# Four adjacent PSUM banks as one tile for a Strassen-type kernel's products, and sums of seven blocks handled as wide operations

## The chip, the cores and the metric

The kernel runs on one core of one Trainium2 chip. The metric is the device time of one execution in microseconds. Three runs of the kernel before took 747.97, 747.55 and 747.0 us, so the median is 747.55 us. The engines are named as the profile names them: PE multiplies (PEld loads its weights), DVE does elementwise vector work, ACT copies and applies functions, POOL does a little housekeeping, SP issues transfers. Products land in PSUM, which has eight banks of 512 fp32 columns in each of 128 partitions.

## What is computed

The reference, cut to what matters, with 8 batches, 8 heads, 576 tokens, head size 64, a model width of 512 and a hidden width of 1024, all in fp32:

```
kv  = einsum('bhsd,bhse->bhde', k, v)
out = einsum('bhsd,bhde->bhse', q, kv)
x   = out / sqrt(mean(out*out, -1) + 1e-6) * g_norm      # then heads side by side: 4608 x 512
a, b = x @ w1, x @ w2
return ((a * b) @ w3) @ w_out
```

## The kernel before

The kernel first multiplies w3 by w_out once (`fold_chunk`, L682: w3o, 1024 x 512, eight sums in two halves of four PSUM banks), because the two last products have nothing between them. Then it goes through nine groups T of 512 tokens: the first 512 of each of the batches 0 to 7, and group 8, which collects the 64 left-over tokens of each batch. The order is 0 to 6, 8, 7. Each group has two stages: the gates, `a * b` for 1024 hidden columns in four parts p0 to p3, and the projection by w3o. Attention for the next batch (k times v, L335; q times kv, L413; left-over tokens, L432) is done in between, in pieces that a list in `steps` places.

Matrix products are not done plainly but with Winograd's form of Strassen's scheme: seven products of quarter blocks and a chain of sums and differences. `winograd` (L705 for its matmuls) runs one level of it. Its seven products are accumulated in three PSUM banks r1, r2, r3, since several of the sums can be made by letting PE add onto what a bank holds: after product 1, ACT copies r1 to SBUF (`keep`, L719, name p1); product 3 is added onto r1 and is copied again (u2); product 5 is added onto r1 and, in most parts, copied (u3); product 7 is added too. Products 2 and 4 share r2, and product 6 has r3. Each result c12, c22, c11, c21 is then a sum of a bank and an SBUF copy, made by DVE (L848) and followed by the multiplication a*b (L849); for c21 ACT copies one half of r1 (L843) and DVE multiplies it with the other half (L845).

From group 1 on the projection (`project_twice`, L1175), and from group 2 on half of the gates (`gates_of_two`, L964, for the parts p0 and p1 together), use two levels: each of the seven products is itself seven small products of 128 x 128, which land as seven blocks in two PSUM banks, four in the first and three in the second. ACT copies them in two instructions (L984 and L985, L1186 and L1187), or DVE adds them onto an SBUF copy in two (L989 and L990, L1214 and L1215), and `finish` turns a sum of seven blocks into a quarter result with four DVE operations (L1001 to L1004, L1196 to L1199), and for the second factor of the gates multiplies (L1006). The inner sums of the left operand are made by DVE in `sum_inner` (L1133 to L1137), four operations for each of the seven products.

The order on PE, POOL and SP is that of the source (`manual_schedule`); in the last part of the gates and the projection that holds for DVE too. Elsewhere a scheduler orders DVE and ACT. Semaphore waits between engines are put in by the framework, which follows who writes and reads which tile. `between` pieces put attention work behind the third and sixth product of a level; `run_slot` puts ACT's half of the transposes behind a certain copy.

PSUM is shared by two pools: `ps_mm` has five tiles of one bank for products, `ps_at` three for attention. Each `bank(ps_mm, "mm")` is a tile of its own and takes over the bank of an older tile once that has been read:

```
    ps_mm = ctx.enter_context(tc.tile_pool(name="ps_mm", bufs=5, space=PSUM))
    ps_at = ctx.enter_context(tc.tile_pool(name="ps_at", bufs=3, space=PSUM))
    def bank(pool, tag):
        return pool.tile([P, 512], FP32, name=tag, tag=tag)
```

## Time and profile before

| what | value |
|---|---|
| median of three runs | 747.55 us |
| span of the profiled execution | 744.3 us |
| what the median has beyond that span | 3.25 us |
| PE busy | 736.6 us, 99% |
| DVE busy | 648.0 us, 87%, 1377 instructions |
| ACT busy | 379.3 us, 51%, 652 instructions |
| mean granted TensorE clock | 1.000 |
| DMA moved | 169.67 MB, mean 228 GB/s |

The profiled execution's own span is 744.3 us from the first to the last instruction; the time of a run has some 3 us of start and end around it. The stages lie as follows in the span: the fold of w3 and w_out to 82.7 us, group 0 to 149, group 1 to 238, groups 2 to 6 about 73 us each to 604.6, groups 8 and 7 about 68 us each, without attention. PE's matmuls count as busy from issue to their modelled end, so that neighbours overlap by some 0.16 us; an fp32 matmul of 128 x 128 starts every 0.223 us and one of 128 x 256 every 0.432 us when nothing holds them (98 of the former in 21.89 us, 24 of the latter in 10.36 us).

### The profile page before, as it was taken

The page shows a single profiled execution, that of the slowest core. Times are in us where ns is not written, and L with a number is a line of the kernel's source. Part 1 is how long each engine was busy: PE and PEld are TensorE (multiplying, and loading weights), DVE is VectorE, ACT ScalarE, POOL GpSimd, SP SyncE. Part 2 cuts the span into 40 slices and gives each one's busy share as a digit, 9 for nine tenths or more (in the row PEclk, how much of TensorE's full clock was granted, in tenths as well). Part 3 has the DMA queues.
Part 4 walks back from the last instruction along what each step waited for, and adds up shares of the span by engine and source line. Part 5 has one row for each costly group of instructions (what it writes and reads, how often), then busy time and mean ns, then how long its engine had stood idle before and what let it go on. Part 6 is the DMA issues. An engine that isn't in the chain of part 4 may idle for free.

```text
span 744.3 us, 16995 instructions
## 1 busy us (share of the span) xinstructions
PE 736.6 (99%) x6843; PEld 657.9 (88%) x6843; DVE 648.0 (87%) x1377; ACT 379.3 (51%) x652; POOL 22.4 (3%) x29
## 2 busy tenths in 40 slices
PE   8999999999999999999999999999999999999998
PEld 5455788888899999999999999999999999999997
DVE  7987998967869798989898989898989997898897
ACT  6787868415553575356536753575267323222421
POOL 0000000132000000010000000000001000000000
PEclk9999999999999999999999999999999999999999
DMA  9997934499997789678967896679757662465454
GB/s 316 367 304 220 256 103 126 122 337 301 285 294 291 213 221 274 264 200 244 276 237 208 255 291 243 213 240 264 254 141 220 215 217 87 163 227 163 135 198 136
DMA packets 135458, 169.67 MB, mean 228 GB/s; under 512 B 78036, under 2 KB 110804, under 8 KB 135380
## 3 DMA queue, kind: packets, MB, share of 16 engines
q1 hardware_dynamic: 132928, 154.16, 68.0%
q10 hardware_dynamic: 2452, 14.42, 5.6%
q8 instruction: 54, 0.88, 0.5%
q14 instruction: 24, 0.20, 0.1%
HBM read 130.55 MB, written 20.71 MB: 203 GB/s over the span
## 4 chain that ended last, share of the span: by engine, by line
PE 95%; DVE 2%; DMA 2%; ACT 0%; issue 0%; SPq 0%; ACTq 0%; DVEq 0%
PE mm L705 37%; PE mm L1175 23%; PE mm L964 21%; PE mm L682 7%; PE at L335 2%; PE at L413 1%; DMA raw<-in_moe_w_out_dram 1%; PE mm L413 1%; PE at L669 1%; DVE ab L162 1%; DVE w_sb L172 0%; PE at L1226 0%; DMA raw<-in_moe_w_dram 0%; DVE c L848 0%; PE at L432 0%
## 5 line engine op out<-in xcount | busy, mean ns | idle before, releaser
L705 PE MATMUL mm<-xT,w_sb 128*128 128x256 f32 x480 | 110.2, 379 | 0.0
L705 PEld LDWEIGHTS mm<-xT,w_sb 128*128 128x128 f32 x480 | 90.3, 190 | 12.2 <-issue 0.5
L705 PE MATMUL mm<-xc,ws 128*128 128x256 f32 x352 | 79.6, 379 | 0.0
L705 PEld LDWEIGHTS mm<-xc,ws 128*128 128x128 f32 x352 | 66.9, 190 | 9.1
L682 PE MATMUL mm<-chunks,ab 128*128 128x512 f32 x128 | 60.7, 605 | 0.7 <-DVE chunks L172 0.7
L964 PE MATMUL mm<-ws,w3o_sb 128*128 128x128 f32 x350 | 53.9, 275 | 0.0
L719 ACT COPY u<-mm 128x512 f32<-128x512 f32 x38 | 22.3, 586 | 58.0 <-PE mm L705 31.0
L1186 ACT COPY u<-mm 128x512 f32<-128x512 f32 x23 | 13.5, 586 | 75.3 <-DVE raw L1199 44.0
L1175 PE MATMUL mm<-w3o_sb,ab 128*128 128x128 f32 x368 | 48.6, 275 | 0.0
L719 ACT COPY p<-mm 128x512 f32<-128x512 f32 x46 | 27.0, 588 | 41.6 <-PE mm L705 26.6
L1175 PE MATMUL mm<-w3o_sb,raw 128*128 128x128 f32 x372 | 48.1, 275 | 0.0
L964 PEld LDWEIGHTS mm<-ws,w3o_sb 128*128 128x128 f32 x350 | 46.4, 192 | 0.0
L1175 PEld LDWEIGHTS mm<-w3o_sb,ab 128*128 128x128 f32 x368 | 45.4, 192 | 0.4
L1175 PEld LDWEIGHTS mm<-w3o_sb,raw 128*128 128x128 f32 x372 | 44.8, 192 | 0.0
L705 PE MATMUL mm<-xc,w_sb 128*128 128x256 f32 x176 | 42.5, 384 | 0.9 <-ACT u L719 0.9
L381 DVE TENSOR_REDUCE inv<-sq 128x8 f32<-128x512 f32 (+1 forms) x40 | 24.6, 629 | 21.1 <-ACT sq L380 21.1
L682 PEld LDWEIGHTS mm<-chunks,ab 128*128 128x128 f32 x128 | 21.6, 190 | 22.4 <-issue 14.4
L705 PE MATMUL mm<-xT,ws 128*128 128x256 f32 x160 | 38.5, 384 | 0.0
L705 PEld LDWEIGHTS mm<-xc,w_sb 128*128 128x128 f32 x176 | 32.7, 190 | 6.2 <-ACT u L719 1.7
L843 ACT COPY c<-mm 128x256 f32<-128x256 f32 x22 | 8.2, 371 | 53.9 <-PE mm L705 53.9
L308 ACT COPY xT<-xn 128x1024 uint16<-128x1024 uint16 x28 | 32.5, 1168 | 2.3 <-DMA xn<-xT 2.3
L705 PEld LDWEIGHTS mm<-xT,ws 128*128 128x128 f32 x160 | 29.8, 190 | 4.2
(250 smaller groups left out, 1745.9 us busy)
## 6 DMA issues: line engine op xcount, KB each, us to landing
w3o_sb<-w_l SPq DMA_DIRECT2D x21, 896.0 KB, 5.4
w3o_sb<-w3o_l SPq DMA_DIRECT2D x18, 896.0 KB, 5.1
raw<-in_moe_w_dram SPq DMA_DIRECT2D x31, 512.0 KB, 7.6
raw<-w3o_l SPq DMA_DIRECT2D x15, 896.0 KB, 4.7
w3o_sb<-w3o_l ACTq DMA_DIRECT2D x14, 896.0 KB, 5.0
k_sb<-in_k_dram SPq DMA_DIRECT2D x16, 576.0 KB, 4.7
v_sb<-in_v_dram SPq DMA_DIRECT2D x16, 576.0 KB, 5.9
q_sb<-in_q_dram SPq DMA_DIRECT2D x32, 256.0 KB, 3.5
```

The source lines that it names most:

```text
L162: nc.vector.scalar_tensor_tensor(out=low_bits, in0=hi, scalar=0x80000000, in1=low_bits, op0=ALU.bitwise_and, op1=ALU.bitwise_or,)
L308: copy(words(dst), src)
L335: nc.tensor.matmul(ps[r * D:(r + 1) * D, :], lhsT=k_sb[rows, r, cols], rhs=v_sb[rows, r, cols], start=(j == 0), stop=(j == JS - 1),)
L381: adds["norm"] = nc.vector.tensor_reduce(out=inv[:, i], in_=sq.rearrange("p (h d) -> p h d", d=D), axis=AX.X, op=ALU.add)
L413: nc.tensor.matmul(o_ps[l][tokens, n * D:(n + 1) * D], lhsT=qT[r][rows, e, i, tokens], rhs=kv_b[rows, m // 2 ^ l, e, h, :], start=True, st ...
L682: nc.tensor.matmul(sums_ps[half][m], lhsT=w3T[half, c][:, m, :], rhs=chunks[:, c, 1, :], start=(c == 0), stop=(c == KF - 1),)
L705: nc.tensor.matmul(ps[:, u, :], lhsT=lhsT(a_name, u, c), rhs=rhs(b_name, c),  start=(u == 0 and c == 0 and to is None), stop=(c == chunks ...
L719: copies.setdefault(name, []).append(nc.scalar.copy(t, ps))
L843: copied = nc.scalar.copy(c, one[:, 0, :])
L964: nc.tensor.matmul(ps[place // 4][:, place % 4, :], lhsT=x, rhs=y, start=new and place // 4 not in seen, stop=True, skip_group_check=True,)
L1175: nc.tensor.matmul(to[:, i, :], lhsT=x[:, c, :], rhs=y[:, c, :], start=new and place // 4 not in seen, stop=(c == 1), skip_group_check=True,)
L1186: nc.scalar.copy(t[:, 0:4], ps[0])
```

## The change

The five product tiles of one bank become one tile `mm` of four adjacent banks, allocated once, and the attention pool gets four banks. A counter (`next_unit`) alternates between the two halves. A `winograd` takes both banks of its half for r1 and r2 and the second bank of the other half for r3; the two-level stages use one half for r1 and the other for r2, so that seven blocks are 896 adjacent columns and are copied or added in one instruction each. The SBUF copies live in three adjacent slots, so that two of them can be finished by one set of wide operations (`finish_two_sums`); `sum_inner` makes the inner sums for two products at a time where their operands are adjacent; `sum_ab_two` covers three parts instead of two. In the gates the second factor's result is made in place in its slot. k times v of the next batch moves from the last part of the gates of groups 2 to 5 to the place of the batch's second attention product. All attention products use the attention pool. The multiplications, their operands and their order on PE are otherwise the same: 3466 matmuls before and after. The diff, cut to its core (the same edits to `keep`, `add` and `finish` are made in `project_twice`):

```diff
-    ps_mm = ctx.enter_context(tc.tile_pool(name="ps_mm", bufs=5, space=PSUM))
-    ps_at = ctx.enter_context(tc.tile_pool(name="ps_at", bufs=3, space=PSUM))
+    ps_mm = ctx.enter_context(tc.tile_pool(name="ps_mm", bufs=1, space=PSUM))
+    ps_at = ctx.enter_context(tc.tile_pool(name="ps_at", bufs=4, space=PSUM))
+    mm = ps_mm.tile([P, 4, 512], FP32, name="mm")
+    def next_unit():
+        units.append(len(units) % 2)
+        return units[-1]
+    def two_banks(k):
+        return mm[:, 2 * k:2 * k + 2, :].rearrange("p b (i n) -> p (b i) n", n=P)
...
-    ab = [const.tile([P, NF, 2, N], FP32, name=f"ab{i}") for i in range(2)]
+    ab_all = const.tile([P, 2, NF, 2, N], FP32, name="ab")
+    ab = [ab_all[:, i] for i in range(2)]
...
-            sums_ps[half] = [bank(ps_mm, "mm") for m in range(NH)]
+            sums_ps[half] = [mm[:, m, :] for m in range(NH)]
...
         if more:
-            fs[6 if in_two else second].append((batch(b + 1).begin_kv, 0))
+            fs[second].append((batch(b + 1).begin_kv, 0))
...
     # winograd
-            ps = to if to is not None else bank(ps_mm, "mm").rearrange("p (u n) -> p u n", u=2)
+        unit = next_unit()
+        r1, r2, r3 = (
+            mm[:, i, :].rearrange("p (u n) -> p u n", u=2)
+            for i in (2 * unit, 2 * unit + 1, 2 * (1 - unit) + 1)
+        )
...
     # gates_of_two
-            nc.scalar.copy(t[:, 0:4], ps[0])
-            run_slot(at, nc.scalar.copy(t[:, 4:7], ps[1][:, 0:3]))
+            run_slot(at, nc.scalar.copy(z, ps[:, 0:7]))
...
-            nc.vector.tensor_add(z[:, 0:4], ps[0], z[:, 0:4])
-            nc.vector.tensor_add(z[:, 4:7], ps[1][:, 0:3], z[:, 4:7])
+            nc.vector.tensor_add(z, ps[:, 0:7], z)
...
-            r1, r3, r2 = ([mm[i] for i in pair] for pair in plan[w])
+            unit = next_unit()
+            r1, r2 = two_banks(unit), two_banks(1 - unit)
...
+    def finish_two_sums(z, dst, multiply=False):
+        def wide(i):
+            return z[:, :, i:i + 1].to_broadcast([P, 2, 2, P])
+        ...
+        nc.vector.tensor_add(z[:, :, 6], z[:, :, 6], z[:, :, 0])
+        nc.vector.tensor_add(z[:, :, 4:6], z[:, :, 4:6], wide(6))
+        nc.vector.tensor_add(to_1, z[:, :, 1:3], wide(4))
+        last = nc.vector.tensor_add(to_0, z[:, :, 3:6:2], z[:, :, 0:3:2])
...
-        c11, c12, c21, c22 = (ab[i][:, 0:2, j, :] for i in range(2) for j in range(2))
-        s1, s2, s4 = (t[:, 0:2] for t in ab_sums)
+        c11, c12, c21, c22 = (ab[i][:, 0:NF - 1, j, :] for i in range(2) for j in range(2))
+        s1, s2, s4 = (t[:, 0:NF - 1] for t in ab_sums)
...
     # the last part of the gates
-                        lambda: sum_inner(0, lambda: all_of(f() for f in (sum_2, sum_3))),
-                        lambda: sum_inner(1),
+                        lambda: sum_inner(0, between=lambda: all_of(f() for f in (sum_2, sum_3))),
+                        lambda: sum_inner(1, 2),
...
                     following["c22"].append(of_two[0])
-                    following["c21"].append(of_two[1])
+                    following["c11"].insert(1, of_two[1])
```

More of the change, by code (lines that the diff above doesn't have):

```diff
@@ L85, in bank @@
         return pool.tile([P, 512], FP32, name=tag, tag=tag)
+    mm = ps_mm.tile([P, 4, 512], FP32, name="mm")
+    units = []
+    def next_unit():
[3 more added lines that the diff above has]
+        return mm[:, 2 * k:2 * k + 2, :].rearrange("p b (i n) -> p (b i) n", n=P)
     loaded, copies, adds = {}, {}, {}
@@ L271, in keep_warm @@
     def keep_warm(n):
-        t = bank(ps_mm, "mm")
+        t = bank(ps_at, "at")
         for _ in range(n):
@@ L399, in product @@
         def product(h):
-            of_mm = b and not (h and b > FIRST_OF_TWO)
-            o_ps = [bank(*((ps_mm, "mm") if of_mm else (ps_at, "at"))), bank(ps_at, "at")]
+            o_ps = [bank(ps_at, "at") for _ in range(2)]
             for m in range(4):
@@ L570, in turns_by_scalar @@
                 at(("p3", "u2"), begin, ("q", b + 1, r), n.q_by_dma, r)
-                at(("proj", ("u2", "u3")[r]), end, ("q", b + 1, r))
+                at(("proj", "u2"), end, ("q", b + 1, r))
     def steps(b):
@@ L691, with late_slots @@
     tick = const.tile([P, 1], FP32, name="tick")
-    def late_tile(name):
-        return late_pool.tile([P, 7, P], FP32, name=name[0] if name[0] == "u" else name)
+    sums_in_slots = []
+    def late_slots(a, n=1):
+        return sums_in_slots[0][:, a] if n == 1 else sums_in_slots[0][:, a:a + n]
     def winograd(
@@ L698, in winograd, with product @@
     ):
-        def product(a_name, b_name, to=None):
-            ps = to if to is not None else bank(ps_mm, "mm").rearrange("p (u n) -> p u n", u=2)
+        unit = next_unit()
[3 more added lines that the diff above has]
+        )
+        def product(a_name, b_name, ps, new=True):
             for u in range(2):
@@ L708, in product @@
                         rhs=rhs(b_name, c),
-                        start=(u == 0 and c == 0 and to is None),
+                        start=(u == 0 and c == 0 and new),
                         stop=(c == chunks - 1),
@@ L714, in product @@
             after()
-            return ps
         def keep(name, ps):
-            t = late_tile(name)[:, 0:4, :].rearrange("p (u a) n -> p u (a n)", u=2)
+            if name == "p1":
+                t = pair_of_sums[:, 0].rearrange("p s c t -> p (s c) t")
+            else:
+                t = late_slots(2 if name == "p5" else 1)
+            t = t[:, 0:4, :].rearrange("p (u a) n -> p u (a n)", u=2)
             copies.setdefault(name, []).append(nc.scalar.copy(t, ps))
@@ L722, in keep @@
             return t
-        r1 = product("a11", "b11")
+        product("a11", "b11", r1)
         p1 = keep("p1", r1)
-        r2 = product("s1", "t1")
+        product("s1", "t1", r2)
         p5 = keep("p5", r2)
-        product("s2", "t2", r1)
+        product("s2", "t2", r1, False)
         u2 = keep("u2", r1)
         between()
-        product("s4", "b22", r2)
+        product("s4", "b22", r2, False)
         done("c12", r2, u2)
-        product("s3", "t3", r1)
+        product("s3", "t3", r1, False)
         done("c22", p5, keep("u3", r1) if keep_u3 else r1)
-        r3 = product("a12", "b21")
+        product("a12", "b21", r3)
         done("c11", r3, p1)
         between()
-        product("a22", "t4", r1)
+        product("a22", "t4", r1, False)
         done("c21", r1, None)
@@ L772 @@
     o_sbs, ab_sums, w3o_sums, streams, inner_sums, in_a_row = [], [], [], [], [], []
+    two_ab_sums, two_o_sbs = [], []
     PART = 7 * 2 * P
@@ L779, in allocate @@
             free["w", p] = late_pool.tile([P, 3, 2, h, P], FP32, name=f"ws{p}")
+        sums_in_slots.append(late_pool.tile([P, 3, 7, P], FP32, name="slots"))
     def allocate_projection():
@@ L788, in allocate_projection @@
         ab_sums.extend(blocks[0:3])
+        two_ab_sums.append(room[0].rearrange("p (s f n) -> p s f n", s=2, n=N))
         w3o_sums.extend(blocks[3:6])
         o_sbs.extend(t.rearrange("p (m j) t -> p m (j t)", m=2) for t in blocks[6:8])
+        two_o_sbs.append(room[3].rearrange("p (h m n) -> p h m n", h=2, m=2))
         for p in range(NF):
@@ L936, in gates_of_two @@
     def gates_of_two(T, between=lambda: None):
-        mm = [bank(ps_mm, "mm").rearrange("p (i n) -> p i n", n=P) for _ in range(5)]
-        plan = [((0, 1), (2, 3), (4, 2)), ((3, 4), (2, 0), (1, 2))]
-        names = [("p1", "p5", "u2", "p1"), ("u2", "p5", "p1", "u2")]
+        places = [(0, 1, 2, 0), (2, 0, 1, 2)]
         def products(n, w, ps, new):
@@ L964, in products @@
                 nc.tensor.matmul(
-                    ps[place // 4][:, place % 4, :], lhsT=x, rhs=y,
+                    ps[:, place, :], lhsT=x, rhs=y,
                     start=new and place // 4 not in seen, stop=True, skip_group_check=True,
@@ L971, in products @@
                 between()
-            return ps
         def load(w, n):
@@ L980, in load, with keep @@
                     load_b()
-        def keep(name, ps, at):
-            t = late_tile(name)
-            nc.scalar.copy(t[:, 0:4], ps[0])
-            run_slot(at, nc.scalar.copy(t[:, 4:7], ps[1][:, 0:3]))
-            return t
+        def keep(slot, ps, at):
+            z = late_slots(slot)
+            run_slot(at, nc.scalar.copy(z, ps[:, 0:7]))
+            return z
         def add(z, ps):
-            nc.vector.tensor_add(z[:, 0:4], ps[0], z[:, 0:4])
-            nc.vector.tensor_add(z[:, 4:7], ps[1][:, 0:3], z[:, 4:7])
+            nc.vector.tensor_add(z, ps[:, 0:7], z)
         def finish(z, w, i, j):
-            def wide(i):
-                return z[:, i:i + 1].to_broadcast([P, 2, P])
-            dst = ab[i][:, 0:2, j, :].rearrange("p m (n t) -> p m n t", t=P)
-            to = dst
-            if w:
-                to = late_pool.tile([P, 2, N], FP32, name="c").rearrange("p m (n t) -> p m n t", t=P)
-            nc.vector.tensor_add(z[:, 6], z[:, 6], z[:, 0])
-            nc.vector.tensor_add(z[:, 4:6], z[:, 4:6], wide(6))
-            nc.vector.tensor_add(to[:, 1], z[:, 1:3], wide(4))
-            nc.vector.tensor_add(to[:, 0], z[:, 3:6:2], z[:, 0:3:2])
-            if w:
-                nc.vector.tensor_mul(dst, dst, to)
+            finish_sums(z, ab[i][:, 0:2, j, :].rearrange("p m (n t) -> p m n t", t=P), w)
         for w in range(2):
-            r1, r3, r2 = ([mm[i] for i in pair] for pair in plan[w])
-            of_p1, of_u2, of_p5, of_last = names[w]
+            unit = next_unit()
+            r1, r2 = two_banks(unit), two_banks(1 - unit)
+            of_p1, of_u2, of_p5, of_last = places[w]
             products(0, w, r1, True)
             p1 = keep(of_p1, r1, (w, 0))
-            products(1, w, r3, True)
-            add(p1, r3)
+            products(1, w, r2, True)
+            add(p1, r2)
             finish(p1, w, 0, 0)
@@ L1021, in gates_of_two @@
             add(p5, r1)
-            finish(p5, w, 1, 1)
             products(5, w, r2, False)
             add(z, r2)
-            finish(z, w, 0, 1)
+            both = ab_all[:, :, 0:2, 1, :].rearrange("p i m (n t) -> p i m n t", t=P)
+            finish_two_sums(late_slots(of_u2, 2), both, w)
             products(6, w, r1, False)
@@ L1028, in gates_of_two, with finish_sums, wide @@
         loaded_w.clear()
+    def finish_sums(z, dst, multiply=False):
+        def wide(i):
+            return z[:, i:i + 1].to_broadcast([P, 2, P])
+        to_0, to_1 = (z[:, m:m + 4:3] for m in range(2)) if multiply else (dst[:, m] for m in range(2))
+        nc.vector.tensor_add(z[:, 6], z[:, 6], z[:, 0])
+        nc.vector.tensor_add(z[:, 4:6], z[:, 4:6], wide(6))
+        nc.vector.tensor_add(to_1, z[:, 1:3], wide(4))
+        last = nc.vector.tensor_add(to_0, z[:, 3:6:2], z[:, 0:3:2])
+        if multiply:
+            made = z[:, 0:6].rearrange("p (n k) t -> p k n t", n=2)[:, 0:2]
+            last = nc.vector.tensor_mul(dst, dst, made)
+        return last
+    def finish_two_sums(z, dst, multiply=False):
+        def wide(i):
+            return z[:, :, i:i + 1].to_broadcast([P, 2, 2, P])
+        to_0, to_1 = (
+            (z[:, :, m:m + 4:3] for m in range(2)) if multiply else (dst[:, :, m] for m in range(2))
+        )
+        nc.vector.tensor_add(z[:, :, 6], z[:, :, 6], z[:, :, 0])
+        nc.vector.tensor_add(z[:, :, 4:6], z[:, :, 4:6], wide(6))
+        nc.vector.tensor_add(to_1, z[:, :, 1:3], wide(4))
+        last = nc.vector.tensor_add(to_0, z[:, :, 3:6:2], z[:, :, 0:3:2])
+        if multiply:
+            for i in range(2):
+                made = z[:, i, 0:6].rearrange("p (n k) t -> p k n t", n=2)[:, 0:2]
+                last = nc.vector.tensor_mul(dst[:, i], dst[:, i], made)
+        return last
     def sum_ab_two():
-        c11, c12, c21, c22 = (ab[i][:, 0:2, j, :] for i in range(2) for j in range(2))
-        s1, s2, s4 = (t[:, 0:2] for t in ab_sums)
+        c11, c12, c21, c22 = (ab[i][:, 0:NF - 1, j, :] for i in range(2) for j in range(2))
+        s1, s2, s4 = (t[:, 0:NF - 1] for t in ab_sums)
         return [
@@ L1123, with sum_inner @@
     inner = {}
-    def sum_inner(n, between=lambda: None, place=None):
-        s1, s2, s4 = ab_sums
-        x = [ab[0][:, :, 0], s1, s2, s4, ab[0][:, :, 1], ab[1][:, :, 0], ab[1][:, :, 1]][n]
+    def sum_inner(*ns, between=lambda: None):
+        x_1 = ab[1].rearrange("p f j n -> p j f n")
+        if ns == (1, 2):
+            x = two_ab_sums[0]
+        elif ns == (5, 6):
+            x = x_1
+        else:
+            n, = ns
+            x = {0: ab[0][:, :, 0], 3: ab_sums[2], 4: ab[0][:, :, 1], 6: x_1[:, 1]}[n].unsqueeze(1)
         a11, a12, a21, a22 = (
-            x[:, 2 * j:2 * j + 2, i * P:(i + 1) * P] for i in range(2) for j in range(2)
+            x[:, :, 2 * j:2 * j + 2, i * P:(i + 1) * P] for i in range(2) for j in range(2)
         )
-        s1, s2, s4 = inner_sums[(n if place is None else place) % 3]
+        if len(ns) == 2:
+            s1, s2, s4 = (pair_of_sums[:, :, i] for i in range(3))
+        else:
+            s1, s2, s4 = (
+                t.unsqueeze(1) for t in (
+                    inner_sums[n % 4 // 3] if n < 6 else [pair_of_sums[:, 0, i] for i in range(3)]
+                )
+            )
         nc.vector.tensor_add(s1, a21, a22)
@@ L1137, in sum_inner @@
         nc.vector.tensor_sub(a21, a11, a21)
-        inner[n] = [a11, a12, a22, s1, s2, s4, a21]
+        for i, n in enumerate(ns):
+            inner[n] = [t[:, i] for t in (a11, a12, a22, s1, s2, s4, a21)]
     def project_twice(T, last, ahead, load_after):
@@ L1151, in store, with products @@
                     )
-        def products(n, ps=None):
-            new = ps is None or n == 5 or last and n == 6
-            if ps is None:
-                ps = [bank(ps_mm, "mm").rearrange("p (i n) -> p i n", n=P) for _ in range(2)]
+        unit = next_unit()
+        r1, r2 = two_banks(unit), two_banks(1 - unit)
+        def products(n, ps):
+            new = n in (0, 1, 5) or last and n == 6
             a11, a12, a22, s1, s2, s4, s3 = inner[n]
@@ L1172, in products @@
             ):
-                to, i = ps[place // 4], place % 4
                 for c in range(2):
                     nc.tensor.matmul(
-                        to[:, i, :], lhsT=x[:, c, :], rhs=y[:, c, :],
+                        ps[:, place, :], lhsT=x[:, c, :], rhs=y[:, c, :],
                         start=new and place // 4 not in seen,
@@ L1181, in products, with finish_right @@
                     seen.add(place // 4)
-            return ps
         def keep(name, ps):
-            t = late_tile(name)
-            nc.scalar.copy(t[:, 0:4], ps[0])
-            run_slot(("proj", name), nc.scalar.copy(t[:, 4:7], ps[1][:, 0:3]))
-            return t
+            z = late_slots({"p1": 0, "p5": 2}.get(name, 1))
+            run_slot(("proj", name), nc.scalar.copy(z, ps[:, 0:7]))
+            return z
         def finish(z, half, j):
-            def wide(i):
-                return z[:, i:i + 1].to_broadcast([P, 2, P])
             dst = o_sbs[half][:, :, j * N:(j + 1) * N].rearrange("p m (i n) -> p m i n", n=P)
-            nc.vector.tensor_add(z[:, 6], z[:, 6], z[:, 0])
-            nc.vector.tensor_add(z[:, 4:6], z[:, 4:6], wide(6))
-            nc.vector.tensor_add(dst[:, 1], z[:, 1:3], wide(4))
-            adds["out"] = nc.vector.tensor_add(dst[:, 0], z[:, 3:6:2], z[:, 0:3:2])
+            adds["out"] = finish_sums(z, dst)
             if not last:
-                if j == 0:
-                    store(half)
+                store(half)
             elif (half, j) != (0, 0):
                 store_block(half, j)
+        def finish_right():
+            dst = two_o_sbs[0][:, :, :, N:2 * N].rearrange("p h m (i n) -> p h m i n", n=P)
+            finish_two_sums(late_slots(1, 2), dst)
         def store_block(half, j, a=0, b=2, queue=nc.sync):
@@ L1213, in add @@
         def add(z, ps):
-            nc.vector.tensor_add(z[:, 0:4], ps[0], z[:, 0:4])
-            nc.vector.tensor_add(z[:, 4:7], ps[1][:, 0:3], z[:, 4:7])
+            nc.vector.tensor_add(z, ps[:, 0:7], z)
         done[T] = len(done)
@@ L1236, in project_twice @@
             load_b()
-        r1 = products(0)
+        products(0, r1)
         p1 = keep("p1", r1)
         load_b()
-        sum_inner(2)
-        r2 = products(1)
+        products(1, r2)
         p5 = keep("p5", r2)
@@ L1254, in project_twice @@
         if last:
-            sum_inner(6, place=5)
+            sum_inner(6)
             finish(p1, 0, 0)
             add(z, r2)
-        else:
-            add(z, r2)
-            sum_inner(5)
-        finish(z, 0, 1)
-        products(4, r1)
-        if last:
-            add(p5, r1)
-        z = keep("u3", r1)
-        load_after()
-        if not last:
-            sum_inner(6)
-            nc.vector.tensor_add(p5, p5, z)
-        finish(p5, 1, 1)
-        products(6 if last else 5, r2)
-        load_after()
-        if last:
+            finish(z, 0, 1)
+            products(4, r1)
+            add(p5, r1)
+            z = keep("u3", r1)
+            load_after()
+            finish(p5, 1, 1)
+            products(6, r2)
+            load_after()
             add(z, r2)
@@ L1279, in project_twice @@
         else:
+            add(z, r2)
+            sum_inner(5, 6)
+            products(4, r1)
+            add(p5, r1)
+            load_after()
+            finish_right()
+            products(5, r2)
+            load_after()
             add(p1, r2)
@@ L1394 @@
     kv_sb.append(late_pool.tile([P, 2, 2, NP // 2, D], FP32, name="kv_sb2"))
+    pair_of_sums = late_pool.tile([P, 2, 3, 2, P], FP32, name="inner_sums")
     in_first_group = True
@@ L1433 @@
             gates(T, p, between)
-            run(sum_ab(p))
             if T in TWICE:
@@ L1528 @@
         preparing_w, prepared, replaced, begun_p = prepare_w(), [], [], []
-        third = late_pool.tile([P, 3, 2, P], FP32, name="inner_sums")
-        inner_sums.append([third[:, i] for i in range(3)])
-        in_a_row.append({"s1": third.rearrange("p s c t -> p (s c t)")})
+        in_a_row.append({"s1": pair_of_sums[:, 1].rearrange("p s c t -> p (s c t)")})
 _INS = ['q', 'k', 'v', 'g_norm', 'moe_w1', 'moe_w2', 'moe_w3', 'moe_w_out']
```

## The prediction

> **What bounds the kernel now.** I read the page first, busy shares and chain together.

> ```profile
> PE 736.6 (99%) x6843; PEld 657.9 (88%) x6843; DVE 648.0 (87%) x1377; ACT 379.3 (51%) x652; POOL 22.4 (3%) x29
> ...
> PE 95%; DVE 2%; DMA 2%; ACT 0%; issue 0%; SPq 0%; ACTq 0%; DVEq 0%
> PE mm L705 37%; PE mm L1175 23%; PE mm L964 21%; PE mm L682 7%; PE at L335 2%; PE at L413 1%; DMA raw<-in_moe_w_out_dram 1%; PE mm L413 1%; PE at L669 1%; DVE ab L162 1%; DVE w_sb L172 0%; PE at L1226 0%; DMA raw<-in_moe_w_dram 0%; DVE c L848 0%; PE at L432 0%
> ```

> PE is the chain, and it does not stand still. The view of waits, for PE alone, holds everything that it waited for:

> ```profile
> PE mm L275 <- POOL ident masks.py:199: 1.4, 1, 1.4
> PE at L669 <- DVE chunks L172: 1.3, 2, 0.8
> PE mm L705 <- ACT u L719: 0.9, 2, 0.7
> PE mm L682 <- DVE chunks L172: 0.7, 1, 0.7
> ```

> So DVE and ACT, however many instructions they save, can give nothing but the 0.9 us of the third row. What the change can take is another matter: it lies in who holds PE. The same 0.9 us are also the only place where the trace shows what a hold costs. Next, therefore, the timeline around 122 us (start, length, instruction), first PE, then ACT:

> ```profile
> 117.98 3.62 PE L705 MATMUL mm<-xT,w_sb 128*128 128x256 f32 x16
> 122.27 0.91 PE L705 MATMUL mm<-xc,w_sb 128*128 128x256 f32 x3 [0.67 <-ACT u L719]
> ...
> 121.63 0.59 ACT L719 COPY u<-mm 128x512 f32<-128x512 f32 x1 [0.36 <-PE mm L705]
> ```

> Eight matmuls from 117.98 would let the next start at 117.98 + 8*0.432 = 121.44. PE had to wait for the copy, which began 0.03 us after PE's end at 121.60 and ended at 122.22; PE went on 0.05 us later, at 122.27. The hold costs 0.83 us: 0.16 of lost overlap, 0.03, the copy, 0.05. For DVE the pieces are in two rows of the timeline (PE ends at 245.50, DVE starts at 245.61) and three of the chain (DVE ends at 18.07, PE starts at 18.11):

> ```profile
> 243.61 1.89 PE L705 MATMUL mm<-xT,ws 128*128 128x256 f32 x8
> ...
> 245.61 0.69 DVE L848 TENSOR_TENSOR c<-mm,u 128x512 f32<-128x512 f32 x1
> ```
> ```profile
> 16.83 1.24 DVE chunks L172
> 18.07 0.04 issue
> 18.11 0.66 PE at L669 x4
> ```

> Groups of instructions (busy us, mean ns) give the lengths:

> ```profile
> L984 ACT COPY p<-mm 128x512 f32<-128x512 f32 x35 | 20.6, 587 | 24.0 <-PE mm L964 20.5 <-DVE p L990 3.3
> L985 ACT COPY p<-mm 128x384 f32<-128x384 f32 x35 | 17.0, 486 | 1.3
> L990 DVE TENSOR_TENSOR p<-mm,p 128x384 f32<-128x384 f32 x28 | 15.4, 550 | 0.0
> L848 DVE TENSOR_TENSOR c<-mm,u 128x512 f32<-128x512 f32 x22 | 15.1, 686 | 11.3 <-PE mm L705 11.2
> L1271 DVE TENSOR_TENSOR p<-p,u 128x896 f32<-128x896 f32 x7 | 7.6, 1084 | 0.0
> ```

> **The one tile, part by part.** In the kernel before, each bank is a tile; PE's waits on ACT and DVE are for a bank that it will itself overwrite or for an operand. In the changed kernel's instruction stream, as built, this is different: 322 times the first matmul of a product waits for an ACT copy or a DVE operation that reads *another* bank of `mm`, namely the product before. Product 2 of a `winograd` (second bank) waits for the copy of product 1 (first bank), product 3 for the copy of product 2, product 5 for the add of c12, and so on; likewise in the two-level stages. The framework orders writers and readers of a PSUM tile as a whole. The double buffering is gone: product, reader, product, reader. Behind each waiting matmul stand all later products and the attention matmuls in PE's order; ACT and DVE, in turn, wait for PE.

> The count by reader, less those with attention matmuls in between (0.6 to 2.2 us of PE work that hides the reader), by the price:

> - ACT, 512 columns (L719 copies, the eight of the fold): 94 - 6 = 88, at 0.84: 73.9 us.
> - ACT, 896 columns: 88 - 5 = 83. From 486 ns for 384 and 587 for 512 a copy of 896 is 0.89 to 0.91, so 0.16 + 0.04 + 0.91 + 0.05 = 1.16: 96.3 us. Between 0.84 (no longer than 512) and 1.32 (both old copies in a row, 1.07); I take the line through them.
> - DVE add, 512: 54 - 7 = 47, at 0.16 + 0.10 + 0.69 + 0.04 = 0.99: 46.5 us.
> - DVE add, 896: 64 - 3 = 61. The 896-wide row has 1.084, so 1.39: 84.8 us, and 2 for the three that a left-over product half hides.
> - c21's multiplication: 22. In nine places ACT's 0.37 and DVE's 0.41 follow the product: 1.1 each, 9.9. In five, behind attention's norm, as in the trace: PE goes on at 252.86, L845 ends at 254.60: 1.8 each, 9.0. Before the two-level projections (eight) it is late, below: 41.5.

> Late, because DVE's order is the source's, and two wide steps now stand ahead of it. Before (timeline of DVE):

> ```profile
> 289.22 0.68 DVE L848 TENSOR_TENSOR c<-mm,p 128x512 f32<-128x512 f32 x1
> ...
> 292.33 0.42 DVE L1137 TENSOR_TENSOR ab<-ab 128x256 f32<-128x256 f32 x1
> ...
> 294.25 0.41 DVE L845 TENSOR_TENSOR ab<-c,mm 128x256 f32<-128x256 f32 x1
> ```

> From the end of c11's add (289.90) to 292.75 are 2.85 us of first inner sums; then s4 of `sum_ab_two` over 768 columns (0.95, between 0.69 and 1.08), the inner sums of two products at once (four operations of 512, 0.71 with their gaps: 2.85) and the multiplication, 0.42: 7.07. Before, nobody waited for it. Now the projection's first matmul does, while PE has only product 7 (1.73) to do: 7.07 + 0.05 - 1.78 = 5.3 in seven groups, 4.4 in group 1, which has no s4.

> Sum of holds: 73.9 + 96.3 + 46.5 + 86.8 + 60.4 = 364 us.

> **Queues.** A reader can stand behind other work. In the last gate part the copy u waits for a slot that `finish` of the two-level gates still reads, about 0.9 in seven groups: 6. In group 0 DVE was busy for 23.4 of the 24.15 us from 82.85; twelve adds behind half a conversion (0.6): 7. In the fold ACT was busy 75%: 8 holds by 0.75*0.58: 4. Together 17; at least 0, at most 85, if ACT's 171 copies each met half a 1.17 us transpose copy at 51% (51) and DVE's adds half an operation (17).

> **Gains.** PE's order has the same 3466 matmuls. k times v moved to the product: alone they cost 1.29 (PE would go on at 282.04, does at 283.33) and 1.18 (269.31 to 270.49), together 2.23 (248.80 to 251.03): 0.24 less, four times, 0.96. The transfers that it issues on SP come earlier and land in 4.7 to 5.9 us, a group ahead of their use: nothing. The two old holds of 0.9 are in the count above. DVE has 231 instructions less (1146), ACT 102 less; adds of 896 take 1.08 instead of 0.69 + 0.55, wide finishes save similarly. All of it lay under PE, so it is costed at nothing; while PE stands, only the length of the one reader counts. The pair of inner sums is covered by product 4 of the projection (3.12 against 2.85).

> **Sum.** 744.3 + 364 + 17 - 1.9 = 1123, and 3.25 outside the span: 1127 us. Low end, if the 279 simple holds lose no overlap (0.16 each, -45) and queues cost nothing (-17): 1065. High end 1195.

> [...]

> **Rivals.**

> *Only same-bank waits hold* (0.06). Then the late c21 still blocks: the projection's second product writes its bank. It would start 4.85 us after product 7 started, c21 is done 8.6 after (add end at 1.55, plus 7.07): 3.8 in seven groups, 2.6 in group 1, so 29 us and 775. For it: c21 read a bank that nobody needed soon. Against it: the built waits.

> *Not slower: readers overlap products after all* (0.04). If PE's next product runs while its predecessor's bank is read, as all of the trace shows it for separate tiles, and c21 comes in time, only the gains are left: 747.55 - 0.96 - 0.9 = 745.7. It decides if a reader ends within PE's 0.16 us of overlap; at 0.59 it cannot.

> *PE slows as well* (0.06). With holds after each product PE may run at the pace of its first stretch: 14 matmuls from 1.35 to 6.00, 0.332 each instead of 0.223.

> ```profile
> 1.35 4.81 PE L275 MATMUL mm<-ident 128*128 128x128 f32 x28 [1.35 <-POOL ident masks.py:199]
> ```

> On all of PE's 737 us that is +360: about 1490; after the eight long holds alone, 14 matmuls each, 1.5*8 = 12: 1139, inside the range. Against the first: after 0.67 and 0.76 us of idling the pace did not drop. [...]

> **How the numbers follow.** The forecast has 0.84, at 1127. The range 1060 to 1210 takes in both ends of handoffs and queues and a few slow stretches; outside lie the rivals and a little. 0.2% (1.5 us) is about what a measurement can tell from no change: slower 0.96, and the last rival, 0.25% faster, is split: 0.02 and 0.02.

> **What would show it.** Right: PE's busy share falls to about two thirds with its busy time near 735; its waits name the copies (L739, L1005, L1240) with some 0.6 to 1.0 us each and the adds (L872, L1009, L1264), and L869 with eight of about 5 us; groups 2 to 5 take about 115 us instead of 73; DVE's instructions are 1146. Wrong: PE above 90% busy, no waits on L739, or matmuls further apart than 0.223 and 0.432 us inside a product.

## The result, and the profile after

The changed kernel takes 1181.1 us (median of four runs, 1178.7 to 1182.8) against 747.7: 1.581 times as long, 95% interval 1.578 to 1.584. Its profiled execution has a span of 1180.8 us, 436.5 more than before. The page first: span, busy shares, granted clock by slice, chain by engine.

```profile
span 1180.8 us, 16519 instructions
...
PE 845.5 (72%) x6843; PEld 680.5 (58%) x6843; DVE 639.3 (54%) x1146; ACT 363.6 (31%) x550; POOL 20.5 (2%) x29
...
PEclk9997999979899999999999999989999999999999
...
PE 52%; DVE 15%; ACT 12%; issue 2%; DMA 1%; DVEq 0%; ACTq 0%
```

DVE and ACT do a little less work than before, and yet they now hold 27% of the chain. PE is idle for 1180.8 - 845.5 = 335.3 us, where it was idle for 7.7, and its busy time has grown by 108.9 with the same matmuls. The view of PE's waits (total us, times, longest) names who it stands behind:

```profile
PE mm L986 <- DVE slots L1009: 49.4, 42, 1.3
PE mm L986 <- ACT slots L1005: 46.3, 44, 1.5
PE mm L722 <- DVE c L872: 40.6, 45, 3.4
PE mm L722 <- ACT slots L739: 40.1, 57, 1.2
PE mm L1230 <- DVE ab L869: 36.8, 8, 4.7
PE mm L1230 <- ACT slots L1240: 26.8, 25, 2.1
PE mm L1230 <- DVE slots L1264: 26.7, 22, 1.3
```

These are the readers of products, each 22 to 57 times with some 0.7 to 1.2 us, and L869, c21's multiplication, eight times with 4.6. One such place in the timeline, PE first, then DVE (start, length, instruction):

```profile
424.91 1.99 PE L722 MATMUL mm<-xc,w_sb 128*128 128x256 f32 x8 [0.78 <-DVE c L872]
431.61 2.34 PE L1230 MATMUL mm<-w3o_sb,ab 128*128 128x128 f32 x12 [4.70 <-DVE ab L869]
433.74 2.44 PE L1230 MATMUL mm<-w3o_sb,raw 128*128 128x128 f32 x12
436.02 0.61 PE L1230 MATMUL mm<-w3o_sb,ab 128*128 128x128 f32 x4
437.62 1.60 PE L1230 MATMUL mm<-raw 128*128 128x128 f32 x12 [0.99 <-ACT slots L1240]
439.07 1.50 PE L1230 MATMUL mm<-raw,inner_sums 128*128 128x128 f32 x12
```
```profile
427.62 0.95 DVE L1078 TENSOR_TENSOR raw<-ab,raw 128x768 f32<-128x768 f32 x1
...
429.93 0.69 DVE L1189 TENSOR_TENSOR inner_sums<-raw,inner_sums 128x512 f32<-128x512 f32 x1
430.54 0.68 DVE L1191 TENSOR_TENSOR raw<-raw 128x512 f32<-128x512 f32 x1
431.14 0.41 DVE L869 TENSOR_TENSOR ab<-c,mm 128x256 f32<-128x256 f32 x1
```

PE's product 7 ends at 426.9. c21 could be multiplied then, but DVE has the end of the first inner sums, the sum over 768 columns (L1078) and the pair of inner sums (L1187 to L1191) in front of it; L869 ends at 431.55 and PE goes on at 431.61. Something else is in these rows: twelve instructions of the projection (each matmul stands in these rows as two) take 2.34 and 2.44 us, and a little later 1.60 and 1.50. Busy time by stretches of 3.41 us (PE, PEld, DVE, ACT, POOL, then the granted clock) shows why:

```profile
428.87:432.28 3.41, 0.67 (x6) 0.67 (x7) 3.27 (x7) 0.00 (x0) 0.00 (x0) 1.00 0.00 0
432.28:435.69 3.41, 3.41 (x19) 3.41 (x18) 1.81 (x5) 0.00 (x0) 0.00 (x0) 0.50 0.00 0
435.69:439.10 3.41, 2.42 (x21) 2.23 (x21) 2.22 (x5) 1.96 (x2) 0.00 (x0) 1.00 0.36 84
```

In the first stretch PE is idle for 2.74 us; in the next its clock is halved. The same follows each of the eight long holds, for one stretch of 3.41 us in five places and for two in three. The wait is paid for twice.

### The profile page after: what moved, and what is told of

Same layout as the page of the kernel before. It is cut to its first block, busy times and chain, and to the rows that moved or that the text cites. A ratio compares the mean times of both kernels' runs of the same rounds, so it can differ in the third digit from the quotient of the medians.

```text
span 1180.8 us, 16519 instructions
## 1 busy us (share of the span) xinstructions
PE 845.5 (72%) x6843; PEld 680.5 (58%) x6843; DVE 639.3 (54%) x1146; ACT 363.6 (31%) x550; POOL 20.5 (2%) x29
## 4 chain that ended last, share of the span: by engine, by line
PE 52%; DVE 15%; ACT 12%; issue 2%; DMA 1%; DVEq 0%; ACTq 0%
PE mm L722 20%; PE mm L1230 17%; PE mm L986 14%; DVE slots L1009 4%; ACT slots L1005 4%; ACT slots L739 2%; ACT slots L1240 2%; DVE c L872 2%; DVE slots L1264 2%; DVE inv L392 1%; ACT sq L391 1%; PE at L346 1%; ACT inner_sums L739 1%; ACT kv_sb L356 1%; DMA w3o_sb<-w3o_l 1%
## 5 line engine op out<-in xcount | busy, mean ns | idle before, releaser
L722 PE MATMUL mm<-xT,w_sb 128*128 128x256 f32 x480 | 124.7, 405 | 58.0 <-DVE c L872 25.7
L722 PEld LDWEIGHTS mm<-xT,w_sb 128*128 128x128 f32 x480 | 89.3, 196 | 91.4 <-DVE c L872 36.5
L722 PE MATMUL mm<-xc,ws 128*128 128x256 f32 x352 | 93.1, 410 | 30.9 <-ACT inner_sums L739 15.7
L1009 DVE TENSOR_TENSOR slots<-mm,slots 128x896 f32<-128x896 f32 x42 | 45.9, 1092 | 123.5 <-PE mm L986 96.4
L1240 ACT COPY slots<-mm 128x896 f32<-128x896 f32 x32 | 29.0, 905 | 240.8 <-PE mm L1230 224.4
L1005 ACT COPY slots<-mm 128x896 f32<-128x896 f32 x56 | 50.6, 904 | 166.1 <-PE mm L986 166.1
L1230 PE MATMUL mm<-w3o_sb,ab 128*128 128x128 f32 x368 | 61.1, 319 | 55.1 <-DVE ab L869 36.8
L722 PEld LDWEIGHTS mm<-xc,ws 128*128 128x128 f32 x352 | 66.5, 199 | 57.8 <-ACT inner_sums L739 25.2
L739 ACT COPY slots<-mm 128x512 f32<-128x512 f32 x61 | 35.7, 585 | 152.4 <-PE mm L722 152.3
L1264 DVE TENSOR_TENSOR slots<-mm,slots 128x896 f32<-128x896 f32 x24 | 26.2, 1092 | 92.8 <-PE mm L1230 92.8
L872 DVE TENSOR_TENSOR c<-mm,slots 128x512 f32<-128x512 f32 x22 | 15.2, 691 | 101.1 <-PE mm L722 88.3
L986 PE MATMUL mm<-xT,w_sb 128*128 128x128 f32 x144 | 25.6, 300 | 41.4 <-ACT slots L1005 32.3
L1230 PEld LDWEIGHTS mm<-w3o_sb,raw 128*128 128x128 f32 x340 | 47.9, 220 | 10.8 <-ACT slots L1240 10.8
L722 PE MATMUL mm<-xc,w_sb 128*128 128x256 f32 x176 | 43.9, 392 | 12.4 <-DVE c L872 12.4
L722 PE MATMUL mm<-xT,ws 128*128 128x256 f32 x160 | 39.9, 392 | 12.0 <-ACT slots L739 12.0
L986 PE MATMUL mm<-xc,w3o_sb 128*128 128x128 f32 x154 | 29.2, 294 | 26.5 <-DVE slots L1009 17.5
L986 PEld LDWEIGHTS mm<-xT,w_sb 128*128 128x128 f32 x144 | 18.8, 190 | 49.5 <-ACT slots L1005 38.1
```

Of the source, the lines that this page charges most:

```text
L722: nc.tensor.matmul(ps[:, u, :], lhsT=lhsT(a_name, u, c), rhs=rhs(b_name, c),  start=(u == 0 and c == 0 and new), stop=(c == chunks - 1), s ...
L739: copies.setdefault(name, []).append(nc.scalar.copy(t, ps))
L872: adds.setdefault(name, []).append(nc.vector.tensor_add(c, one, two))
L986: nc.tensor.matmul(ps[:, place, :], lhsT=x, rhs=y, start=new and place // 4 not in seen, stop=True, skip_group_check=True,)
L1005: run_slot(at, nc.scalar.copy(z, ps[:, 0:7]))
L1009: nc.vector.tensor_add(z, ps[:, 0:7], z)
```

## The experiments

Nine kernels were run. None leaves out or changes any of the arithmetic (e8 adds matmuls whose results nobody reads); times are medians.

**The tile alone.** Two kernels start from the kernel before, with its narrow instructions and its order. Both give the products four banks and attention four, with the bank numbers of the two-level gates written for four banks, and differ in one thing: the four product banks are slices of one tile, or four tiles.

```diff
+    mm_tile = ps_mm.tile([P, 4, 512], FP32, name="mm")          # e2
+    mm_tiles = [ps_mm.tile([P, 512], FP32, name=f"mm{i}") for i in range(4)]   # e3
+    def mm_bank():
+        ring.append(len(ring) % 4)
+        return mm_tile[:, ring[-1], :]                          # e2;  e3: mm_tiles[ring[-1]]
...
-            o_ps = [bank(*((ps_mm, "mm") if of_mm else (ps_at, "at"))), bank(ps_at, "at")]
+            o_ps = [bank(ps_at, "at") for _ in range(2)]
...
-            ps = to if to is not None else bank(ps_mm, "mm").rearrange("p (u n) -> p u n", u=2)
+            ps = to if to is not None else mm_bank().rearrange("p (u n) -> p u n", u=2)
```

> The kernel before with its narrow instructions and its order, but its product banks are slices of one tile of four banks (attention has the other four). Theory (whole-tile order is the loss): every reader holds PE. 88 copies of 512 at 0.84 (74), 83 pairs of copies at 0.16+0.04+0.59+0.49+0.08=1.36 (113), 47 adds of 512 at 1.02 (48), 61 pairs of adds at 0.16+0.11+0.69+0.55+0.05=1.56 (95), c21 elsewhere 19, c21 before the eight projections at 4.6 (37), the fold's eight at 1.5 (12): 398; and 56 for slower matmuls, as the changed kernel's trace has them: 747.6+398+56, about 1200 us (1140 to 1270), somewhat above the changed kernel, since two narrow readers take longer than one wide. Rival (the wide operations or their order are the loss): 745 to 770.

> The same as the run with one tile, except that the four product banks are four tiles of one bank. Theory: only the order of the whole tile costs; four banks instead of five are enough, since each bank's reader has the length of the next product (1.56 to 3.1 us) to finish: 747 to 755 us. Rival (four banks instead of five, or attention's products in the same four banks, are what holds PE): more than 770 us, with waits at the first matmul of a product for the reader of its own bank.

One tile: 1181.7 us (two runs), 1.583 [1.580, 1.585]. Four tiles: 789.2, 1.057 [1.056, 1.058]. So 392.6 of the 435 us by which e2 is slower than the kernel before hang on one declaration, with not one wide operation in the kernel. The theory's size for e2, 1200, was 18 too high. For e3 the theory's 747 to 755 is missed: the rival came true, that four banks are too few, at 42 us. PE's waits of e3 (where L851 is c21's multiplication):

```profile
PE mm L1181 <- DVE ab L851: 19.0, 8, 2.4
PE mm L711 <- DVE ab L851: 5.3, 3, 2.4
PE mm L970 <- DVE ab L851: 4.0, 7, 0.7
```

A part takes three banks; with five, the next stage begins in two others. With four, the projection's first product already needs the bank of which c21 is still to be made, and waits 2.4 us for it. With the overlap that each wait loses the three rows cost 31 us; matmuls at half clock lost another 8 (the mean granted clock is 0.989).

**The tile in the changed kernel.** All wide operations stay; the four banks become two tiles of two, and a one-level part alternates between them.

```diff
-    mm = ps_mm.tile([P, 4, 512], FP32, name="mm")
+    mm = [ps_mm.tile([P, 2, 512], FP32, name=f"mm{k}") for k in range(2)]
...
-            mm[:, i, :].rearrange("p (u n) -> p u n", u=2)
-            for i in (2 * unit, 2 * unit + 1, 2 * (1 - unit) + 1)
+            mm[k][:, i, :].rearrange("p (u n) -> p u n", u=2)
+            for k, i in ((unit, 0), (1 - unit, 0), (1 - unit, 1))
```

> The changed kernel with all its wide operations, but the four banks are two tiles of two banks, and a one-level part alternates between the tiles from product to product (r1 in one, r2 and r3 in the other). Theory: a reader now has the next product's time; what is left is c21's multiplication before the projection, which is done 7.07 us after c11's add and which the projection's second product now waits for, 3 to 3.8 us in seven groups and 2.6 in group 1: 24 to 29 us, 746+27, about 773 us (758 to 790); PE's waits name L869 with about 3.5 us, eight of them, and hardly anything else. Rival (wide reads of two banks disturb PE, or wide operations come too late): more than 800 us, with matmuls further apart than 0.223 and 0.432 us or with waits on the wide copies and adds.

832.1 us, 1.113 [1.111, 1.116]: 349 us come back, but 59 more remain than the theory allowed, and the rival's bound of 800 is passed. PE's waits:

```profile
PE mm L1230 <- DVE ab L869: 23.8, 8, 3.1
PE mm L722 <- ACT slots L739: 12.1, 7, 2.1
PE mm L722 <- DVE slots L1009: 6.4, 5, 1.3
PE mm L722 <- DVE c L872: 6.3, 6, 1.7
PE mm L692 <- ACT w3o_sb L697: 3.2, 4, 1.5
```

The first row is the one that was foreseen, 3.1 instead of 3 to 3.8. The others, and 2.2 for c21 in group 1, are readers that come later than one product's time: 30 us that the expectation did not have, and 34 with the overlap that each wait loses. Most of the rest is the clock: 41 us of the span were granted half (mean granted clock 0.975), and the matmuls in them took 18 us longer; at 320.88 us, behind a wait of 3.14 us for L869, twelve instructions of the projection took 2.93 us, where they take 1.60 at full clock (0.52 was granted from 319.80 to 326.70 us). Of the rival's two causes, disturbed matmuls are not seen: outside the half-clock stretches the matmuls keep their pace, but for 0.10 us on the first after a wait (from 298.05 us, after a wait of 1.31, eight instructions took 1.99 us and the next sixteen 3.62; in the kernel before 1.89 and 3.62). Wide operations that come too late are seen: the row of L1009 is a wide add, and L869 stands behind two wide steps.

**c21 earlier, then the slot.** In e5 c21's multiplication goes ahead of the two wide steps in DVE's order, with the two tiles. e6 also puts the one-level copy p5 into another slot.

```diff
                         lambda: sum_inner(0, between=lambda: all_of(f() for f in (sum_2, sum_3))),
-                        lambda: sum_inner(1, 2),
                     ],
-                    "c21": [sum_4],
+                    "c21": [lambda: sum_inner(1, 2), sum_4],
...
-                    following["c11"].insert(1, of_two[1])
+                    following["c21"].insert(0, of_two[1])
...
-                t = late_slots(2 if name == "p5" else 1)        # e6
+                t = late_slots(0 if name == "p5" else 1)        # e6
```

> The kernel with two tiles, and in DVE's order c21's multiplication stands ahead of the last sum of sum_ab_two, the pair of inner sums and sum_4. Theory: in the run with two tiles the eight projections waited 23.8 us for L869, plus 1 of lost overlap, and the half-clock stretches right after these waits (six, 27.3 us long, half of it lost) cost about 14; the pair of inner sums now comes some 0.3 us late in seven groups (2): 832.1-25-14+2, about 795 us (782 to 805), no L869 wait at a projection, and a granted clock of 1.0 in the projections. Rival (the time of those waits goes to the inner sums, which are now behind c21): above 820 us, with waits of about 3 us at the projection's second product.

> As the run with two tiles and c21 early, and the one-level copy p5 goes into slot 0 instead of slot 2, which the last finish of the two-level gates still reads. Theory: the copy p5 then need not wait for that finish (it ends 1.8 us later than the one on slot 0), so the seven waits of 1.2 to 2.1 us at L722 for L739 (12.1 us, and 1.1 of lost overlap) and the half clock after two or three of them (5) go: 18 us less than the run before, about 777 us. Rival (it is ACT, busy with transposes, that makes this copy late, not the slot): no more than 5 us less, the same waits.

797.8 us (1.067 [1.065, 1.070]) and 780.2 (1.044 [1.042, 1.046]): 34 and 18 us less, as expected. The projections' waits for L869 are gone in e5 and nothing took their place; the loss by half clock fell from 18 to 3 us (mean granted clock 0.995). In e6 the seven waits for L739 are gone too, and the mean granted clock is 1.000. So it was the slot and not ACT that held this copy. Of what is left, 33 us over the kernel before, these waits are 18, and 21 with the overlap that they lose:

```profile
PE mm L722 <- DVE slots L1009: 6.4, 5, 1.3
PE mm L722 <- DVE c L872: 6.3, 6, 1.7
PE mm L692 <- ACT w3o_sb L697: 3.2, 4, 1.4
PE mm L722 <- DVE ab L869: 2.2, 1, 2.2
```

**c21 earlier in the changed kernel, and work in its hold.** e7 makes the same move of c21 with the one tile. e8 leaves the changed kernel's order and gives PE something to do while it waits.

```diff
         if done[T]:
             load_b()
+        keep_warm(20)                                           # e8
         products(0, r1)
```

> The changed kernel with its one tile, only c21's multiplication ahead of the last sum of sum_ab_two, the pair of inner sums and sum_4. Theory: the hold before the eight projections falls from 4.87 to about 2.6 us, as in the run with four tiles, where c21 stands in the same place (idle 2.43): 18 us; and the half clock after it (15.4 us lost in the projections) goes in at least half of the cases: 8 to 15. Together 26 to 33 less than 1181.1, about 1151 us. If only the hold falls and the half clock stays: 1163. Rival (late c21 does not set the end, its wait is taken over by the inner sums): 1175 to 1185.

> The changed kernel with 20 more 128 x 128 matmuls (20 by 0.223 = 4.46 us) into an attention bank ahead of each projection, where PE waits 4.87 us for c21. The holds stay as they are; only PE isn't idle in them. Theory (the granted clock halves because PE stood idle): no half clock in the projections (37.5 us of it in the changed kernel, in which the first products lost 15.4 us): about 1166 us. Rival (the half clock is not tied to these waits, or comes from the many short holds): the same clock and 1180 to 1184 us, or more by what the fillers hold.

e8: 1165.2 us, 1.559 [1.556, 1.563], 15.9 less than the changed kernel, although PE has 4.6 us more to do in each of eight groups. Its timeline at the place shown above:

```profile
422.90 4.63 PE L286 MATMUL at<-ident 128*128 128x128 f32 x40
427.77 1.60 PE L1230 MATMUL mm<-w3o_sb,ab 128*128 128x128 f32 x12 [0.24 <-DVE ab L869]
429.21 1.50 PE L1230 MATMUL mm<-w3o_sb,raw 128*128 128x128 f32 x12
```

The projection starts no earlier, but at full pace: 1.60 and 1.50 where the changed kernel has 2.34 and 2.44. That the clock was halved there because PE stood idle is shown by this run: from 420 to 445 us its granted clock is 1.00, and over the whole run 0.987 where the changed kernel has 0.969. e7: 1138.6 us, 1.523 [1.520, 1.527], 42.5 less where 26 to 33 were expected. Both parts came, and the first was larger:

```profile
PE mm L1230 <- DVE ab L869: 9.5, 8, 1.2
```

The wait fell from 4.6 to 1.2 (27 us in all), not to the 2.4 of e3: with one tile product 7 starts only after c11's add, about 1 us later (in the changed kernel it waits 0.78 us for it at 424.91 and loses the overlap), so DVE is that much further when product 7 ends. And no projection's first product runs at half clock any more (some 15; the mean granted clock is 0.987). The wide operations do gain a little where PE stands, as a comparison of e2 with the changed kernel shows: PE's waits for adds and copies of the two-level stages are 177 us in e2 and 163 in the changed kernel. There the late c21 (36.8 against 22.2) takes it back, which is why the two times agree.

**k times v alone.** The third part of the change, first in the kernel before (e1), then undone in the changed kernel (e9).

```diff
-            fs[6 if in_two else second].append((batch(b + 1).begin_kv, 0))
+            fs[second].append((batch(b + 1).begin_kv, 0))       # e1; e9 has the reverse
```

> The kernel before with only k times v of the next batch moved beside the batch's second attention product, in four groups. Theory: PE is the chain, and the two pieces together hold 0.24 us less than apart, four times: 0.96 us less, about 746.6 against 747.6. Rival (the piece was hidden or the move costs as much elsewhere): no change, 747.6. Second rival: PE has to wait for k or v, more than 0.5 us longer, with a new row of waits at the k times v matmuls.

> The changed kernel with k times v of the next batch back at its old place, behind the third product of the last part of the gates, in four groups. Theory: with one tile PE stands after each product until its reader is done, and a piece of attention of 1.1 to 1.3 us in that place covers a hold of 0.84 to 1.3, while beside the batch's product, which already covers the hold there, it covers nothing; moving it back costs 0.24 in PE work and hides about 1.0, four times: about 3 us less, 1178 us (1175.5 to 1179.5). Rival (the move is worth its 0.96 us here as in the prediction): 1182 us.

e1: 749.9 us against 746.8, 1.0048 [1.0032, 1.0065]: slower by 3 us, not faster by 1. PE's waits name it:

```profile
PE at L413 <- ACT kv_sb L345: 2.6, 4, 0.7
```

It is not k or v that is missing but, as the order of the rows tells, a bank. With three attention banks, k times v takes two and the product beside it needs two more; at 272.09 us its first two instructions start, and the other 62 wait 0.65 us for the copy that frees the second. In the kernels with four attention banks this row does not appear. With their lost overlap the four waits cost 3.5 us, and one wait for a transfer 0.9; less the 0.96 that was foreseen this is 3.4 of the 3.9 us between the two spans. e9: 1177.6 us, 1.576 [1.573, 1.578] against the changed kernel's 1.581 [1.578, 1.584]: 3.5 us less, as expected, though the intervals touch and single runs overlap. The trace has four waits for a one-level copy fewer, 53 where the changed kernel has 57:

```profile
PE mm L722 <- ACT slots L739: 37.7, 53, 1.4
```

## Why the prediction was right, and where not

**The mechanism** is shown by e2 and e3: one tile for several banks costs 393 us, and the same banks as four tiles do not. "The framework orders writers and readers of a PSUM tile as a whole" was read from the instruction stream, and the time follows that. e4 shows that readers of other tiles' banks do run beside PE: its ACT copy at 300.08 us (0.59 us) lies within PE's sixteen instructions from 299.88 (3.62 us).

**The prices of a handoff** held. Between PE's unhindered start and its real one the trace has, in medians:

| reader | foreseen | measured |
|---|---|---|
| ACT copy, 512 | 88 at 0.84, 73.9 | 0.84, sum 71.0 (80; the fold's apart) |
| ACT copy, 896 | 83 at 1.16, 96.3 | 1.16, sum 100.7 (83) |
| DVE add, 512 | 47 at 0.99, 46.5 | 1.02, sum 47.9 (45) |
| DVE add, 896 | 61 at 1.39, 86.8 with the half-hidden three | 1.35 to 1.42, sum 86.6 (64) |
| c21, early places | 9.9 and 9.0 | 11.9 (7) and 11.1 (7) |
| c21 before projections | 41.5 | 38.1 (8, median 4.87) |
| the fold | 8 at 0.84, and 4 | 1.07, sum 8.6 (8) |

With single others the holds come to some 383 us, against the 364 for holds and 17 for queues that were foreseen. That these two sums agree is in part luck: queues were a guess between 0 and 85. The copy of 896 took 0.905, inside the 0.89 to 0.91 worked out from two narrower ones.

**The step that was mis-sized** is the duration of the matmuls themselves, which the sum left as it was. They took about 56 us longer, which accounts for the 54 between 1127 and 1181. Two things make it up, found by comparing each matmul's distance to the next with its usual pace. The first matmul after a wait takes 0.10 longer (with 256 columns 483 ns instead of 379): 287 times, 29 us. The prediction's own row had this, and the price of a hold left it out: the three instructions from 122.27, right after a wait, took 0.91 us, where the pace of 0.216 each and the end that neighbours overlap make 0.81. And matmuls in stretches of half clock (granted 0.50; 0.969 in the mean of the span) lost 27 us, some 16 of them in the projections (e8). The rival "PE slows as well" had slower matmuls at the right place with 12. It looked at the eight long holds alone; four stretches between the end of the fold and group 1's projection (up to 13.65 us long) came on top. The 0.332 us per matmul that the rival took for a slow pace is itself a mean of two: in the trace of the kernel before, matmuls start 0.427 apart up to 4.4 us and 0.223 apart after. The other version of that rival, the slow pace on all of PE's time, did not happen. A small term was off too: the 3.25 us outside the span are 1.8 in the runs of the changed kernel (1182.58 against a span of 1180.8).

**The signs to look for.** PE's share (72% instead of "about two thirds") and busy time (845 instead of "near 735") missed by the 0.16 us of overlap that each wait turns into busy time, and by the slower matmuls. The waits, their names and sizes, 120 to 121 us from one projection to the next in groups 2 to 6 instead of 115, and 1146 DVE instructions were as described or close to it.

**The gain of 0.96 us** for k times v was wrong in sign. In the changed kernel the piece at its old place covers a reader (e9), which the prediction's count by places overlooked; in the kernel before there is no bank for it (e1). At 3 us it is lost in the sum.

**Fewer DVE and ACT instructions** were costed at nothing while PE is the chain. That is argued from the 0.9 us of waits in the kernel before; no run has the wide operations with five separate banks. What the runs show is that they don't make up for the bank: e6, with every wide operation and a mean granted clock of 1.000, is still 4.4% slower than the kernel before. Four product banks instead of five, as four tiles in e3 and as two in e6, leave 42 and 33 us of waits and slower matmuls. No version here beats the kernel before.

## What to carry to other kernels

A tile is the unit in which a framework may order writers and readers: before banks are joined into one tile to make an operation wider, count how many engines then take turns on it, and keep at least two tiles in turn. Where PE is the chain, as here, one product bank more can be worth more than fewer instructions on the engines beside it. And when PE is made to wait, look at the granted clock behind the wait. Here it fell to half behind each of the changed kernel's eight holds of 4.6 us and behind e4's wait of 3.14 us at 320.88. Such a wait is to be priced twice, once for itself and once for the slower matmuls behind it, or PE is given something harmless to do, which in e8 took 15.9 us off.

## What was not expected of the hardware

| half clock from, us | its length, us | PE idle in it, us | PE idle in the 3.41 us ahead of it |
|---|---|---|---|
| 87.54 | 13.65 | 2.71 | 1.84 |
| 152.39 | 3.41 | 0.12 | 3.14 |
| 203.59 | 3.41 | 0.28 | 3.11 |
| 241.14 | 13.65 | 2.53 | 2.69 |
| 309.40 | 6.83 | 1.13 | 2.71 |
| 432.28 | 3.41 | 0.00 | 2.74 |
| 551.75 | 3.41 | 0.00 | 3.25 |
| 671.22 | 3.41 | 0.31 | 3.41 |
| 790.68 | 6.83 | 0.66 | 3.41 |
| 910.15 | 6.83 | 0.98 | 3.41 |
| 1029.62 | 3.41 | 0.00 | 2.83 |
| 1145.67 | 3.41 | 0.00 | 3.18 |

Ahead of each of them PE stood idle for 1.84 us or more, in one piece or in several: ahead of 87.54 the waits were two, of 0.57 and 1.27 us. The length of the idling alone does not settle it. From 425.46 to 428.87 us PE is idle for 1.96 us, and the clock stays at 1.00 up to 432.28; in e3 PE waits 2.43 us up to 307.38, and the eight instructions behind that take 1.16 us, which is the 1.06 of eight at full clock and 0.10 for the first after a wait. And the half clock lasts longest where PE goes on being idle: in the two stretches of 13.65 us it stands for 2.71 and 2.53 us, in the seven of 3.41 for no more than 0.31. That is a relation read from the records of one kernel; only that idling is the cause was tested (e8).
